# A fused attention and gated feed-forward kernel: the first quad's weight sums made in another stage, wider rows in a DRAM layout, and a new list of steps

## The chip, the cores and the metric

One core of one Trainium2 chip. The metric is the device time of one execution, in microseconds (us). Three executions of the kernel before took 906.19, 904.66 and 909.0 us; the median is 906.19.

## What is computed

Attention for 8 batches and 8 heads over 576 positions of 64 values (heads 0 to 3 see the last 32 positions, heads 4 to 7 every 32nd position before their own), then a gated feed-forward layer over the 8 x 576 = 4608 tokens.

```python
rel = pos[:, None] - pos[None, :]
mask_local = (rel >= 0) & (rel < 32)
mask_strided = (rel >= 0) & (pos[None, :] % 32 == pos[:, None] % 32)
scores = np.where(masks, scale * (q @ k.T), -1e9)        # per batch and head
attn = softmax(scores)
x = (attn @ v).transpose(0, 2, 1, 3).reshape(4608, 512)
gate = 1.0 / (1.0 + np.exp(-(x @ w_gate)))               # w_gate, w_val: 512 x 1536
val = x @ w_val
out = (gate * val) @ w_out                               # w_out: 1536 x 512
```

## The kernel before

**Blocks and stages.** The tokens lie in nine blocks of 512 columns. Every operand of the feed-forward part is split into a high part (rounded to the type fp32r) and a low part (what is left), and a product is made as high x high + high x low + low x high, so a 128 x 128 weight tile against 512 columns gives three matmuls. Blocks 0 to 2 are computed plainly (steps `g`, `v`, `o`). Blocks 3 and 4, 5 and 6, 7 and 8 are computed as pairs, each in two stages, by a scheme that needs seven products of sums where eight would be plain ones. In the first stage of a pair TensorE makes the gate and value products of half the features at a time (`G` and `V`, line 1075, into the banks `p` and `d`); ScalarE copies `p` out (`c`, L1097), VectorE adds `d` (`ad`, L1102), ScalarE makes the sigmoid (`sg`, L1107 and L1110), VectorE multiplies (`mu`, L1116 and L1119) and forms the sums and differences of hidden values that the second stage takes (`ta` to `td`, L1274). In the output stage ScalarE casts a hidden value to its high part (`hx`, L1288), VectorE subtracts for the low part (`hy`, L1292; `hyp` is the same on GpSimd) and TensorE runs `Oa` and `Ob` (L1303). By TensorE's order the first pair's stages run to 494.6 and 554.6 us of the profiled execution, the second pair's output stage begins near 677.

The third pair's gate and value products use a deeper scheme, in four "quads" (n, m): 26 products (`bp`, L1238) of weight sums with x sums. The weight sums are made ahead of time: `bl` loads the 16 words of a quad (128 x 128 each), `bu` makes 33 sums of two words (L1195 on GpSimd; `buv` on VectorE), `bh` casts four of them at a time to a high part on ScalarE (L1203), `bw` makes the low part (L1207, VectorE; `bwp` GpSimd) and `bd` stores both (L1214). The x sums are `xq`, with casts (L1166) and low parts `xw` (L1169; `xwp` on GpSimd). `z` (L726) copies the left-over columns of the attention's output together for them.

**Beside that** run the attention pieces of the pairs to come: scores `S`, masks `M` (L497), softmax steps (`A`, `D`, `U`, `E`, `N`, `W`), transposes `B` (L590), values `X` (L628, L656), and copies out of the banks (`H`, `L`, `R`; L705 is in `R`). The weight sums of the ordinary pairs (`pa`, `pb` L983, `ph`, `pw` L992) are stored to DRAM (`sets`), and TensorE's weights come back from there through the ring: 186 loads of 512 KB, 84 of them from `sets` (`r`, `load_group`).

**What sets the order.** Nothing chooses at run time. `ORDER` lists 3,417 steps by name; each step issues its instructions, and every engine, SyncE with the DMA queue among them, runs its own in the order of the list, waiting by semaphores for what others make. So a step listed between two others stands in the queue of its engine there, and whatever follows on that engine waits with it.

## Time and profile before

| | us | share |
|---|---|---|
| median of three runs | 906.19 | |
| profiled execution | 908.58 | |
| its span in the trace | 906.8 | |
| TensorE busy | 887.7 | 98% |
| VectorE busy | 723.9 | 80% |
| ScalarE busy | 502.2 | 55% |
| GpSimd busy | 464.4 | 51% |
| DMA, mean of 16 engines | | 74% |

The busy time of TensorE is counted from a matmul's begin to its modelled end; matmuls overlap, so a short wait can hide in it. The shares are means over stages of different kinds. The waits of TensorE, and the engines that release them, are the first thing to read.

### The profile page before, as it was taken

What the parts mean: (1) busy time and instruction counts of PE and PEld (TensorE: products, weight loads), DVE (VectorE), ACT (ScalarE), POOL (GpSimd) and SP (SyncE); (2) the same over time, 40 slices, a digit from 0 to 9 for tenths busy, and PEclk for the clock granted to TensorE, in tenths of its full rate; (3) what the DMA queues carried; (4) which work ended last, traced back from release to release, by engine and by line L of the source; (5) the groups of instructions that cost most, each with busy time, mean ns of one, the idle gap of its engine ahead of it and who ended that gap; (6) DMA issues with size and microseconds to landing.
All of it is one profiled execution on the core that took longest, in us unless ns stands there. A gap on an engine that the chain in (4) does not pass through costs nothing.

```text
span 906.8 us, 18603 instructions
## 1 busy us (share of the span) xinstructions
PE 887.7 (98%) x7014; PEld 720.1 (79%) x7014; DVE 723.9 (80%) x1134; ACT 502.2 (55%) x928; POOL 464.4 (51%) x603
## 2 busy tenths in 40 slices
PE   8999989999999999999999999999999999999998
PEld 5788768888887878888778888888877868888886
DVE  6888778776877888789888996768689978998863
ACT  5888754424545555565656664554465554454453
...
GB/s 345 329 238 178 278 280 211 150 199 219 157 227 135 215 215 263 248 310 298 293 266 249 264 237 284 293 292 288 302 321 210 192 281 250 330 234 291 215 213 129
DMA packets 130937, 225.12 MB, mean 248 GB/s; under 512 B 9760, under 2 KB 67104, under 8 KB 130080
## 3 DMA queue, kind: packets, MB, share of 16 engines
...
q8 instruction: 55, 0.90, 0.4%
...
## 4 chain that ended last, share of the span: by engine, by line
PE 80%; DVE 7%; ACT 4%; DMA 4%; issue 2%; POOL 1%; SPq 1%; DVEq 0%; ACTq 0%; POOLq 0%
PE oc L1303 18%; PE p L1075 12%; PE d L1075 10%; PE g L735 9%; PE v L735 8%; PE o L766 7%; PE q L1238 6%; PE qa L1238 2%; PE qv L1238 1%; PE qg L1238 1%; PE s L478 1%; PE x L656 1%; DVE pt L590 1%; DMA quad<-qw 1%; DMA sets<-w 1%
## 5 line engine op out<-in xcount | busy, mean ns | idle before, releaser
L1075 PE MATMUL p<-xs,ring 128*128 128x512 f32 x576 | 141.8, 392 | 4.6 <-issue 2.0
L1075 PEld LDWEIGHTS p<-xs,ring 128*128 128x128 f32 x576 | 107.0, 188 | 28.4 <-issue 2.4
L1075 PE MATMUL d<-xs,ring 128*128 128x512 f32 x432 | 108.4, 395 | 0.1
L1303 PE MATMUL oc<-hh,ring 128*128 128x512 f32 x312 | 104.2, 390 | 0.9 <-DMA ring<-osets 0.5
L1075 PEld LDWEIGHTS d<-xs,ring 128*128 128x128 f32 x432 | 81.9, 190 | 18.2 <-DVE hid L1102 0.5
L766 PE MATMUL o<-w,hh 128*128 128x512 f32 x288 | 90.5, 395 | 0.0
L735 PE MATMUL v<-xh,w 128*128 128x512 f32 x256 | 85.3, 391 | 0.7 <-DVE sb L497 0.6
L735 PE MATMUL g<-xh,w 128*128 128x512 f32 x256 | 85.7, 392 | 0.2 <-ACT e L743 0.2
L983 POOL TENSOR_TENSOR sum<-sum 128x128 f32<-128x128 f32 x100 | 55.6, 558 | 47.3 <-DMA quadw<-sum 32.1
L1195 POOL TENSOR_TENSOR qu<-qw 128x128 f32<-128x128 f32 x96 | 48.7, 525 | 58.9 <-DMA qw<-quadw 45.7
L1303 PE MATMUL oc<-ops,ring 128*128 128x512 f32 x288 | 72.3, 389 | 0.0
L1288 ACT CAST hh<-hid 128x512 fp32r<-128x512 f32 x78 | 47.3, 620 | 40.1 <-PE oc L1303 29.9
L1303 PEld LDWEIGHTS oc<-hh,ring 128*128 128x128 f32 x312 | 58.6, 188 | 13.8 <-DMA ring<-osets 0.9
L1292 DVE TENSOR_TENSOR hl<-hid,hh 128x512 fp32r<-128x512 f32 x55 | 51.9, 962 | 16.8 <-ACT hh L1288 15.2
L1303 PEld LDWEIGHTS oc<-ops,ring 128*128 128x128 f32 x288 | 54.1, 188 | 11.3
L1303 PE MATMUL oc<-hl,ring 128*128 128x512 f32 x156 | 61.3, 393 | 0.8 <-DVE hl L1292 0.6
L766 PEld LDWEIGHTS o<-w,hh 128*128 128x128 f32 x288 | 52.9, 188 | 11.5 <-ACT hh L755 0.2
L978 POOL TENSOR_TENSOR sum<-w 128x256 f32<-128x256 f32 x49 | 40.5, 846 | 39.4 <-DMA sets<-sum 18.8
L590 DVE STREAM_TRANSPOSE pt<-sb 32x320 f32<-32x320 f32 (+1 forms) x112 | 55.4, 495 | 2.9
L735 PEld LDWEIGHTS v<-xh,w 128*128 128x128 f32 x256 | 48.0, 188 | 11.8 <-DVE sb L497 1.0
L735 PEld LDWEIGHTS g<-xh,w 128*128 128x128 f32 x256 | 48.0, 188 | 10.7 <-ACT e L743 0.5
L766 PE MATMUL o<-w,hl 128*128 128x512 f32 x144 | 56.1, 390 | 0.0
...
## 6 DMA issues: line engine op xcount, KB each, us to landing
ring<-sets SPq DMA_DIRECT2D x84, 512.0 KB, 5.6
ring<-osets SPq DMA_DIRECT2D x63, 512.0 KB, 4.5
ring<-quad SPq DMA_DIRECT2D x39, 512.0 KB, 4.8
raw<-in_w_all SPq DMA_DIRECT2D x36, 512.0 KB, 6.1
...
```

What stands on the lines that cost most here:

```text
L478: nc.tensor.matmul(sc[j % len(sc)][g * m : (g + 1) * m, j // len(sc) * BANK + (s - lo) * kk : j // len(sc) * BANK + (s - lo + 1) * kk], q[ ...
L590: nc.vector.transpose(dst[band * LB : (band + 1) * LB, at : at + n, col * LB : (col + 1) * LB], src[part * LB : (part + 1) * LB, x : x + n ...
L735: nc.tensor.matmul(o, w, x, start=first and n == 0, stop=last and n == len(todo) - 1)
L766: nc.tensor.matmul(acc[k][i], h[:, i * P : (i + 1) * P], w, start=f == 0 and n == 0, stop=f == NF - 1 and n == 2,)
L978: by.tensor_tensor(to, part(wh[f][i], c), part(wl[f][i], c), op=ALU.add)
L983: by.tensor_tensor(u[:, to], u[:, x], u[:, y], op=op)
L1075: nc.tensor.matmul(to, w[:, (wi * 2 + c) * P : (wi * 2 + c + 1) * P], x[xi][:, c], start=p in (1, 2, 5) and c == j == 0, stop=c == 1 and j ...
L1195: by.tensor_tensor(to, a, word_slot(w, b), op=ALU.add if op == "+" else ALU.subtract)
L1238: nc.tensor.matmul(quad_bank(m, CHAIN[p]), w[:, wi], xi, start=p in CHAIN_STARTS and j == 0, stop=j == 2, skip_group_check=True)
L1288: nc.scalar.copy(ops[q, p][0], hidden_tile(k, q, KEPT[str(p)]))
L1292: by.tensor_tensor(hl, hidden_tile(k, q, KEPT[str(p)]), hh.bitcast(F32), op=ALU.subtract)
L1303: nc.tensor.matmul(chains[m, at], w[:, (wi * 2 + m) * P : (wi * 2 + m + 1) * P], x[xi], start=p in (1, 2, 5) and q == j == 0, stop=q == PA ...
```

## The change

1. `sets` is laid out so that the two halves (`i`) of a set lie side by side: a ring load reads rows of 4 KB where it read two of 2 KB for each partition.
2. The first quad's words are loaded into two places of the x operands (`w5_0`, `w5_1`) that hold nothing during the first pair's output stage, and its sums are made in three more (`w6_0`, `w6_1`, `w4_0`), instead of in the tiles `xh`, `hh` and `hl` that the output stage uses. The other three quads stay in those tiles.
3. `ORDER` is listed anew. The first quad's load, sums, casts, low parts and stores stand in the first pair's output stage, where they stood in its gate and value stage. In 224 of the 3,417 steps the engine is another: 65 word sums, 24 output low parts and 10 low parts of x sums go from GpSimd to VectorE, 17 output low parts and 23 low parts of words from VectorE to GpSimd, and the rest are a few of each kind. The steps themselves and TensorE's order stay as they were.

```diff
 ORDER = """
...
-v2.10 xd3.0.1 xh3.0.6 xl3.0.6 E11 N11 W11 s2.10 xlp3.1.1 xl3.0.5 g2.11 m2.10 x2.10 po4 B11.3 LV11 v2.11 xlp3.0.2 r3 r2 r4 bl0.0 xdv3.0.2 y2.10 oh2.9.0
...
+hyp3.4.1 ad3.5.0.7 B19.0 pwp5.2.1 B19.2 xh5.1.2 xl5.1.2 G3.5.4 c3.5.1.7 ad3.5.1.7 xh5.0.1 B19.1 V3.5.4 bl0.0 sg3.5.4 mu3.5.4 sg3.5.7 mu3.5.7 G3.5.3
...
-bw1.1.3 hx5.0.1 hy5.0.1 c5.5.0.6 G5.5.7 c5.5.1.6 V5.5.7 xw15 bd1.1.3 ad5.5.0.2 G5.5.5 xu23 bh1.1.4 bw1.1.4 xw23 c5.5.0.7 G5.5.4 r88 bd1.1.4 bu1.1.21
...
+c5.5.0.1 r85 r84 r87 G5.5.2 sg5.4.3 B23.2 X23.1 G5.5.6 bd1.1.2 ad5.5.1.2 V5.5.5 r86 ad5.5.0.2 sg5.5.2 bh1.1.5 bwp1.1.5 V5.5.6 mu5.4.3 c5.5.0.6 mu5.5.2
...
@@ -934,7 +935,7 @@
 
     def sets_of(q):
         if q not in sets:
-            sets[q] = dram.tile([P, 2 * 7, 2, 2, P], F32, name=f"sets{q}")
+            sets[q] = dram.tile([P, 7, 2, 2, 2, P], F32, name=f"sets{q}")
         return sets[q]
 
     def plain_sets(q):
@@ -942,8 +943,8 @@
         for i in range(2):
             for n, w in ((0, wh), (1, wl)):
                 a, b = (w[f][i].bitcast(F32).rearrange("p (k c m) -> p k c m", k=2, c=2) for f in (2 * q, 2 * q + 1))
-                nc.sync.dma_start(sets[q][:, 7 * i : 7 * i + 2, n], a)
-                nc.sync.dma_start(sets[q][:, 7 * i + 2, n], b[:, 1])
+                nc.sync.dma_start(sets[q][:, :2, i, n], a)
+                nc.sync.dma_start(sets[q][:, 2, i, n], b[:, 1])
             for p in W_RAW:
                 k, f = divmod(W_RAW[p], 4)
                 if f // 2 == q % 2:
@@ -996,7 +997,7 @@
         if i == 2:
             to = [out_set(q)[:, 3:7, n, c] for n in range(2)]
         else:
-            to = [sets_of(q)[:, 7 * i + 3 : 7 * i + 7, n, c] for n in range(2)]
+            to = [sets_of(q)[:, 3:7, i, n, c] for n in range(2)]
         nc.sync.dma_start(to[0], h.bitcast(F32))
         nc.sync.dma_start(to[1], u)
 
@@ -1028,7 +1029,7 @@
                 for q in range(2):
                     ring[k, x, 2 * y + q] = to[:, q]
             else:
-                nc.sync.dma_start(to.bitcast(F32), sets[x][:, SLOT[y] : SLOT[y] + 8 : 7].rearrange("p s h c m -> p s (h c m)"))
+                nc.sync.dma_start(to.bitcast(F32), sets[x][:, SLOT[y]].rearrange("p s h c m -> p s (h c m)"))
                 ring[k, x, y] = to
 
     x_set, diffs = {}, {}
@@ -1169,8 +1170,16 @@
         by.tensor_tensor(x_spot(X_AT[n][1]), x_word(f"x{n}"), x_spot(X_AT[n][0]).bitcast(F32), op=ALU.subtract)
 
     def load_words(n, m):
-        w = quad[n, m] = {"w": work.tile([P, 16, P], F32, tag="xh", name=f"qw{n}_{m}")}
-        nc.sync.dma_start(w["w"], quad_words(n, m).rearrange("p q c k m -> p (q c k) m"))
+        from_ = quad_words(n, m).rearrange("p q c k m -> p (q c k) m")
+        if (n, m) == (0, 0):
+            w = quad[n, m] = {i: pool.tile([P, 8, P], F32, tag=f"w5_{i}", name=f"qw{n}_{m}_{i}") for i in range(2)}
+            for i in range(2):
+                nc.sync.dma_start(w[i], from_[:, 8 * i : 8 * i + 8])
+        else:
+            t = work.tile([P, 16, P], F32, tag="xh", name=f"qw{n}_{m}")
+            w = quad[n, m] = {i: t[:, 8 * i : 8 * i + 8] for i in range(2)}
+            nc.sync.dma_start(t, from_)
+        w["sums"] = {}
 
     def word_slot(w, name):
         n = int(name[1:])
@@ -1178,12 +1187,20 @@
             return word_slot(w, ("r3", "r11")[n])
         if name[0] == "r":
             k, f = divmod(n, 4)
-            return w["w"][:, f // 2 * 8 + k % 2 * 4 + f % 2 * 2 + k // 2]
+            return w[f // 2][:, k % 2 * 4 + f % 2 * 2 + k // 2]
         u, at = (5, n % 4 + n // 24 * 2) if n >= 20 else divmod(n, 4)
-        if u not in w:
-            tag = ("hh0", "hl0", "hh1", "hl1", "hh2", "hl2")[u]
-            w[u] = work.tile([P, 4, P], F32, tag=tag, name=f"qu{len(quad)}_{u}")
-        return w[u][:, at]
+        return word_place(w, u)[:, at]
+
+    def word_place(w, u):
+        if u not in w["sums"]:
+            if len(quad) == 1:
+                t = pool.tile([P, 8, P], F32, tag=("w6_0", "w6_1", "w4_0")[u // 2], name=f"qu1_{u // 2}")
+                for j in range(2):
+                    w["sums"][u // 2 * 2 + j] = t[:, 4 * j : 4 * j + 4]
+            else:
+                tag = ("hh0", "hl0", "hh1", "hl1", "hh2", "hl2")[u]
+                w["sums"][u] = work.tile([P, 4, P], F32, tag=tag, name=f"qu{len(quad)}_{u}")
+        return w["sums"][u]
 
     def word_sum(n, m, j, by=nc.gpsimd):
         w = quad[n, m]
@@ -1195,20 +1212,20 @@
             by.tensor_tensor(to, a, word_slot(w, b), op=ALU.add if op == "+" else ALU.subtract)
 
     def word_high_at(w, u):
-        at = (0, 6)[u % 2]
-        return w["w"][:, at : at + 4].bitcast(F32R)
+        return w[u % 4 // 2][:, u % 2 * 4 : u % 2 * 4 + 4].bitcast(F32R)
 
     def word_high(n, m, u):
         w = quad[n, m]
-        nc.scalar.copy(word_high_at(w, u), w[u])
+        nc.scalar.copy(word_high_at(w, u), word_place(w, u))
 
     def word_low(n, m, u, by=nc.vector):
         w = quad[n, m]
-        by.tensor_tensor(w[u].bitcast(F32R), w[u], word_high_at(w, u).bitcast(F32), op=ALU.subtract)
+        x = word_place(w, u)
+        by.tensor_tensor(x.bitcast(F32R), x, word_high_at(w, u).bitcast(F32), op=ALU.subtract)
 
     def store_quad(n, m, u):
         w = quad[n, m]
-        for part, x in ((0, word_high_at(w, u).bitcast(F32)), (1, w[u])):
+        for part, x in ((0, word_high_at(w, u).bitcast(F32)), (1, word_place(w, u))):
             for p, at, size in ((4 * u, 0, 4),) if u < 5 else ((20, 0, 2), (24, 2, 2)):
                 to = place_of(m, p)
                 nc.sync.dma_start(quad_set(n)[:, to // 4, part, to % 4 : to % 4 + size], x[:, at : at + size])
```

Below, names are the program's tiles; a number behind a name tells buffers of one tag apart, and `a<-b,c` is output and inputs.

ScalarE, in the second pair's gate and value stage, around the copy `z` (`xraw8`). Before:

```order
L705 COPY xr6_5732<-x23_7795 128x2x18
L705 COPY xr6_5732<-x23_7795 128x2x12
L705 COPY xr6_5732<-x23_7795 128x2x2
L726 COPY xraw8_7845<-xr0_80 128x4x128
L726 COPY xraw8_7845<-xr2_2135 128x4x256
L726 COPY xraw8_7845<-xr6_5732 128x4x128
L1203 CAST qw1_1_7604<-qu4_2_7608 128x512
L1166 CAST xs7_pt_7858<-xraw8_7845 128x512
L1166 CAST xs7_vv_7880<-xraw8_7845 128x512
L1203 CAST qw1_1_7604<-qu4_3_7611 128x512
L1288 CAST hh5_0_1_7885<-hid5_0_6757 128x512
L1097 COPY e5_5_6_7889<-p05_5_7743 128x512
```

After:

```order
L1111 ACTIVATE e5_5_1_7803<-e5_5_1_7803 128x512
L1219 CAST qw1_1_7559<-qu4_5_7564 128x512
L1098 COPY e5_5_6_7872<-p05_5_7751 128x512
L706 COPY xr6_5718<-x23_7821 128x2x18
L706 COPY xr6_5718<-x23_7821 128x2x12
L706 COPY xr6_5718<-x23_7821 128x2x2
L727 COPY xraw8_7878<-xr0_80 128x4x128
L727 COPY xraw8_7878<-xr2_2269 128x4x256
L727 COPY xraw8_7878<-xr6_5718 128x4x128
L1098 COPY hid5_13_7885<-p15_5_7758 128x512
L1098 COPY e5_5_7_7893<-p05_5_7751 128x512
```

What moved: the copy `e5_5_6<-p05_5`, which empties TensorE's bank `p`, stood behind `z` and five casts, and stands ahead of `z` now; the casts of `xs7` come later.

VectorE, in the first pair's gate and value stage, around the gate product `hid3_10<-e3_4_4,p13_4` (step `mu3.4.4`). Before:

```order
L590 STREAM_TRANSPOSE pt6_2_5809<-sb6_2_5716 32x9x32
L590 STREAM_TRANSPOSE pt6_2_5809<-sb6_2_5716 32x10x32 x2
L1102 TENSOR_TENSOR hid3_11_5722<-hid3_11_5722,d13_4_5669 128x512
L1207 TENSOR_TENSOR qu1_4_4813<-qu1_4_4813,qw0_0_4329 128x512
L1274 TENSOR_TENSOR hid3_7_5380<-hid3_6_5083,hid3_5_5045 128x512
L1102 TENSOR_TENSOR e3_4_6_5714<-e3_4_6_5714,d03_4_5656 128x512
L1116 TENSOR_TENSOR hid3_10_5682<-e3_4_4_5826,p13_4_5649 128x512
L1119 TENSOR_TENSOR hid3_10_5682<-hid3_10_5682,e3_4_1_5689 128x512
L1207 TENSOR_TENSOR qu1_5_4547<-qu1_5_4547,qw0_0_4329 128x512
L1119 TENSOR_TENSOR hid3_11_5722<-hid3_11_5722,e3_4_6_5714 128x512
```

After:

```order
L591 STREAM_TRANSPOSE pt6_2_5746<-sb6_2_5655 32x10x32 x5
L591 STREAM_TRANSPOSE pt6_2_5746<-sb6_2_5655 32x9x32 x2
L591 STREAM_TRANSPOSE pt6_2_5746<-sb6_2_5655 32x10x32
L1103 TENSOR_TENSOR hid3_11_5642<-hid3_11_5642,d13_4_5613 128x512
L1103 TENSOR_TENSOR e3_4_6_5650<-e3_4_6_5650,d03_4_5606 128x512
L1117 TENSOR_TENSOR hid3_10_5603<-e3_4_4_5762,p13_4_5596 128x512
L1309 TENSOR_TENSOR hl3_1_1_5879<-hid3_2_4731,hh3_1_1_5878 128x512
L1120 TENSOR_TENSOR hid3_10_5603<-hid3_10_5603,e3_4_1_5637 128x512
L1120 TENSOR_TENSOR hid3_11_5642<-hid3_11_5642,e3_4_7_5691 128x512
```

What moved: the low parts of the quad's words (`qu1_4`, `qu1_5`) and one hidden sum are gone from here, and the first low part of the output stage (`hl3_1_1`) has come in behind the gate product.

VectorE, in the first pair's output stage (`hl3_...` and `ops3` are low parts that TensorE takes). Before:

```order
L1292 TENSOR_TENSOR hl3_0_2_6157<-hid3_0_4519,hh3_0_2_6156 128x512
L1292 TENSOR_TENSOR hl3_1_2_6139<-hid3_3_4811,hh3_1_2_6138 128x512
L1292 TENSOR_TENSOR ops3_5975<-hid3_5_5045,ops3_5975 128x512
L1274 TENSOR_TENSOR hid3_14_6040<-hid3_13_5983,hid3_12_5961 128x512
L1292 TENSOR_TENSOR hl3_4_2_6182<-hid3_10_5682,hh3_4_2_6181 128x512
L1274 TENSOR_TENSOR hid3_13_5983<-hid3_14_6040,hid3_13_5983 128x512
L1274 TENSOR_TENSOR hid3_5_5045<-hid3_6_5083,hid3_7_5380 128x512
L1292 TENSOR_TENSOR hl3_5_2_6193<-hid3_13_5983,hh3_5_2_6192 128x512
L1274 TENSOR_TENSOR hid3_12_5961<-hid3_14_6040 128x512
L1292 TENSOR_TENSOR ops3_5975<-hid3_2_4764,ops3_5975 128x512
L600 STREAM_TRANSPOSE pt6_3_6055<-sb6_3_5956 32x12x32 x2
```

After:

```order
L1309 TENSOR_TENSOR ops3_5625<-hid3_5_4989,ops3_5625 128x512
L1309 TENSOR_TENSOR hl3_0_2_6110<-hid3_0_4490,hh3_0_2_6109 128x512
L1062 TENSOR_TENSOR xs5_5_1_6118<-xd5_0_0_6043,xs5_5_0_6045 128x512
L1309 TENSOR_TENSOR hl3_4_2_6124<-hid3_10_5603,hh3_4_2_6123 128x512
L1309 TENSOR_TENSOR ops3_5625<-hid3_8_5367,ops3_5625 128x512
L1212 TENSOR_TENSOR qw0_0_1_6015<-qw0_0_0_6014,qw0_0_1_6015 128x128
L1212 TENSOR_TENSOR qw0_0_1_6015<-qw0_0_1_6015 128x128
L1212 TENSOR_TENSOR qu1_2_6129<-qw0_0_1_6015,qw0_0_0_6014 128x128
L1212 TENSOR_TENSOR qu1_2_6129<-qw0_0_1_6015 128x128
L1050 TENSOR_TENSOR xd5_0_2_6142<-xraw6_5682 128x512
L1309 TENSOR_TENSOR hl3_5_2_6150<-hid3_13_5978,hh3_5_2_6149 128x512
L1212 TENSOR_TENSOR qu1_0_6082<-qw0_0_0_6014,qu1_0_6082 128x128
```

What moved: hidden sums (`hid3_...<-hid3_...`) were made between the low parts; now word sums of the quad (`qw0_0_...`, `qu1_...`, 128x128) and a difference of x operands (`xd5_0_2`) stand there.

## Rows read from the trace of the kernel before

**Rows 1.** Page, part 1: busy us (share of the span) and instructions.

```profile
PE 887.7 (98%) x7014; PEld 720.1 (79%) x7014; DVE 723.9 (80%) x1134; ACT 502.2 (55%) x928; POOL 464.4 (51%) x603
```

**Rows 2.** Chain that ended last: start us, us, engine and line, count.

```profile
846.02 57.13 PE oc L1303 x252
```

**Rows 3.** Page, part 5: count, then busy us, mean ns of one, idle and releaser.

```profile
L1303 PE MATMUL oc<-hh,ring 128*128 128x512 f32 x312 | 104.2, 390 | 0.9 <-DMA ring<-osets 0.5
```

**Rows 4.** TensorE's waits: line, waited for, us in total, times, longest.

```profile
PE x L656 <- DMA vv<-in_v_s: 2.4, 1, 2.4
PE p L1075 <- issue: 2.0, 1, 2.0
...
PE p L1075 <- DVE hid L1116: 1.4, 1, 1.4
PE p L1075 <- ACT e L1097: 1.2, 1, 1.2
...
PE x_a L628 <- ACT xr L705: 0.9, 1, 0.9
PE oc L1303 <- DVE hl L1292: 0.6, 2, 0.4
PE v L735 <- DVE sb L497: 0.6, 1, 0.6
...
PE oc L1303 <- ACT hh L1288: 0.4, 1, 0.4
```

**Rows 5.** ScalarE from 662 us in time: start, us, line, operation, tiles.

```profile
662.49 2.11 ACT L726 COPY xraw<-xr 128x512 f32<-128x512 f32 x3
...
667.09 0.60 ACT L1097 COPY e<-p 128x512 f32<-128x512 f32 x1
```

**Rows 6.** VectorE from 474 us in time.

```profile
474.12 0.69 DVE L1207 TENSOR_TENSOR qu<-qu,qw 128x512 fp32r<-128x512 f32 x1
...
475.92 0.68 DVE L1116 TENSOR_TENSOR hid<-e,p 128x512 f32<-128x512 f32 x1
```

**Rows 7.** VectorE at 323.8 us, with the idle time before it.

```profile
323.78 1.18 DVE L992 TENSOR_TENSOR sum<-sum,sumh 128x512 fp32r<-128x512 f32 x1 [1.00 <-ACT sumh L988]
```

**Rows 8.** GpSimd and then ScalarE, from 731 us in time.

```profile
731.44 1.74 POOL L1169 TENSOR_TENSOR xs<-xs,xs 128x512 fp32r<-128x512 f32 x1
...
733.20 0.62 ACT L1166 CAST xs<-xs 128x512 fp32r<-128x512 f32 x1 [3.24 <-POOL xs L1169]
```

**Rows 9.** Page, parts 3 (packets, MB) and 6 (count, KB each, us to landing).

```profile
q8 instruction: 55, 0.90, 0.4%
...
ring<-sets SPq DMA_DIRECT2D x84, 512.0 KB, 5.6
ring<-osets SPq DMA_DIRECT2D x63, 512.0 KB, 4.5
```

**Rows 10.** Windows: us, busy of PE, PEld, DVE, ACT, POOL (count), clock, DMA share, GB/s.

```profile
446.00:450.10 4.10, 4.10 (x130) 3.31 (x129) 4.03 (x7) 3.23 (x7) 1.93 (x2) 1.00 1.00 338
...
452.60:456.60 4.00, 4.00 (x11) 3.16 (x12) 2.31 (x4) 2.14 (x5) 1.55 (x2) 0.58 0.37 113
...
494.60:554.60 60.00, 60.00 (x426) 49.40 (x424) 55.89 (x78) 36.39 (x68) 20.32 (x16) 1.00 0.72 249
554.60:600.00 45.40, 45.40 (x239) 37.44 (x236) 27.13 (x43) 20.27 (x34) 18.75 (x37) 1.00 0.86 298
668.00:737.00 69.00, 67.29 (x289) 53.66 (x289) 61.93 (x70) 37.62 (x70) 44.51 (x29) 1.00 0.68 229
```

**Rows 11.** Groups of VectorE from 494.6 to 554.6 us, shapes apart.

```profile
L1274 DVE TENSOR_TENSOR hid<-hid,hid 128x512 f32<-128x512 f32 x6 | 7.3, 1228 | 0.0
...
L1274 DVE TENSOR_TENSOR hid<-hid 128x512 f32<-128x512 f32 x3 | 2.0, 681 | 0.0
```

**Rows 12.** Groups of the whole span, shapes apart.

```profile
L1195 POOL TENSOR_TENSOR qu<-qw 128x128 f32<-128x128 f32 x96 | 48.7, 525 | 58.9 <-DMA qw<-quadw 45.7 <-PE p L1075 12.7
...
L983 DVE TENSOR_TENSOR sum<-sum 128x128 f32<-128x128 f32 x44 | 15.7, 358 | 1.6 <-DMA quadw<-sum 0.5
```

More of the change, by code (lines that the diff above doesn't have):

```diff
@@ new lines @@
+c3.2.0.6 LV15 G3.2.7 pw2.2.1 pd2.2.1 LQ16 E15 N15 c3.2.0.7 ad3.2.0.7 V3.2.7 Y15 c3.2.1.7 ad3.2.1.7 G3.2.4 sg3.2.4 V3.2.4 pa3.2.0 pb3.2.0 sg3.2.7
+V3.2.3 hx3.2.1 r19 r20 pa3.2.1 G3.2.3 ph3.2.0.0 pwp3.2.0 S16.1 LQ17 pb3.2.1 ta3.1 W15 B15.0 B15.1 R14 B15.3 B15.2 H14 X15.1 Y16 mu3.2.7 G3.3.1
+ad3.2.0.3 mu3.2.4 M16.0 A16 sg3.2.3 D16 ad3.2.1.3 c3.3.0.1 M16.1 H15 G3.3.2 ad3.3.0.2 U16 hy3.2.1 LV16 V3.3.1 c3.3.1.1 G3.3.6 mu3.2.3 r21 r23 E16 N16
+W16 ph3.2.1.1 c3.3.0.6 B16.2 V3.3.6 c3.3.1.6 tav3.2 pwp3.2.1 pd3.2.1 V3.3.2 pa4.2.1 ad3.3.1.2 pb4.2.1 tbv3.1 tc3.2 r22 G3.3.5 G3.3.7 c3.3.0.7 B16.1
@@ new lines @@
+r98 hx5.0.7 hy5.0.7 Oa5.3.5 hyp5.4.5 Ob5.4.5 Ob5.5.5 hx5.1.7 r99 xq17 r100 xu16 tdv5.0 ok5.1.6 Ob5.0.7 hx5.2.7 Oa5.4.5 Oa5.5.5 ok5.0.6 Oa5.0.7 tbv5.5
+xu23 hx5.3.7 td5.1 hx5.5.7 hyp5.5.7 xu1 hy5.1.7 Oa5.1.7 hx5.4.7 Ob5.1.7 xu0 xu5 hx5.0.3 os3.0.7 hy5.2.7 hy5.3.7 Oa5.2.7 Ob5.2.7 hy5.4.7 tdv5.5 hx5.1.3
+hy5.1.3 Oa5.3.7 Ob5.3.7 hy5.0.3 r102 r101 r103 xqv7 xqv15 Ob5.4.7 Ob5.5.7 Oa5.4.7 hx5.2.3 hy5.2.3 ok5.0.5 Oa5.0.3 ok5.1.5 oa5.1.7 os5.1.7 Oa5.1.3
+Oa5.5.7 hx5.3.3 tdv5.2 oa5.0.7 Ob5.0.3 Ob5.1.3 hx5.4.3 xwp0 hx5.5.3 hx5.0.4 hy5.0.4 Ob5.2.3 Oa5.2.3 hyp5.3.3 hx5.1.4 hyp5.4.3 Oa5.3.3 xw23 Oa5.0.4
```

299 lines of the change are left out of this document (146 added, 153 removed).

## The prediction

> **What bounds the kernel now.** I read the share of each engine first, then what TensorE waited for, then the stages in windows, and last the neighbourhood of each wait. TensorE is busy for 887.7 of 906.8 us [rows 1]. The steps that run on it stand in the same order in both lists, with the same shapes, so its work is a constant of this change. What can move is the time in which it stands still: 19.1 us by the busy row. A stop costs a little more than its idle figure: matmuls of 512 columns start every 57.13 / 252 = 0.227 us [rows 2], while one counts as busy for 0.39 us [rows 3], so 0.16 us of each stop hides in "busy". The stops that are named [rows 4]: 2.4 us for a value load (at 130 us), 2.0 us with nothing named (452), 1.4 for VectorE's gate product (476), 1.2 for a copy by ScalarE (667), 0.9 for ScalarE's left-over copy (279), 0.6 for a masked score (325), 0.6 and 0.4 for operands of the output products. The other 9.6 us are start-up, shorter waits and the changes between small and large matmuls; most of these repeat. So the best case is about 2% and no edit can gain more; the worst has no such bound, because any engine can be made late.
>
> The profiled execution took 908.58 us (span 906.8), 2.4 us above the median of the three runs, 906.19. I work out differences on the trace and apply them to the median.
>
> **The change, part by part.** Five of the stops stand behind steps that the new list puts elsewhere.
>
> At 667 TensorE needs a bank that ScalarE empties with the copy `c5.5.0.6`. That copy ran at 667.09, behind the three copies of `z` (2.11 us from 662.49) and five casts [rows 5]. In the new list it stands ahead of `z` and of all five. TensorE then needs nothing that is late there: 1.2 + 0.16 us go. Late next could be `c5.5.1.6`, now behind `z`: its bank is wanted one product of 1.36 us after the other's, about when the copies end, so I count nothing for it; it would cost up to 0.7.
>
> At 476 TensorE waits for the gate product `mu3.4.4`, which VectorE ran at 475.92. Ahead of it stood a low part of the first quad's words, at 474.12 [rows 6], and a hidden sum. Neither stands there now: two starts, 1.2 us of the 1.4, go, half of them because the quad's work left this stage.
>
> At 279 the left-over copy `R5` stood behind the exponential's table load that `D7` makes; now it stands before it. 0.9 us go [rows 4]. At 325 the mask of piece 9 stood behind `pw5.0.0`, 1.18 us that began 1.0 us late on ScalarE [rows 7]; now that step comes after the second masked score and the softmax steps. 0.6 us go.
>
> At 734 ScalarE waited 3.24 us for GpSimd's `xwp0` and the two last casts of the output operands stood behind that wait [rows 8]. Now `hx5.5.4` is listed 12 TensorE steps earlier and GpSimd holds one low part in that stretch instead of six. I count 0.8 us: 0.4 for the cast and 0.4 of the 0.6 for low parts [rows 4].
>
> Sum: 1.2 + 1.2 + 0.9 + 0.6 + 0.8 = 4.7, and 0.16 for each of five stops, 0.8: 5.5 us.
>
> The value load at 130 stays: the store group `pl4` is still ahead of it on SyncE's queue, and only one load of queries (`LQ0`) changes place with it. Bounds 0 and 2.4 us; I take 0.
>
> The longer rows: 84 loads of 512 KB land in 5.6 us from `sets`, where loads of the same size with 4 KB rows, from `osets`, take 4.5 [rows 9]. So each may land 1.1 us earlier. But no wait of TensorE names a load from `sets` [rows 4], so this is hidden and I take 0; the bounds are 0 and what the crowded stretch below is worth.
>
> What is added is in the first pair's output stage, 494.6 to 554.6. VectorE is busy for 55.89 of 60 us there, 4.1 idle [rows 10]. In the list it gets 17 word sums of 128 columns (0.358 each by its nearest row, 6.1), 6 low parts of words (0.68 as the plain sum of 512 columns, 4.1), two low parts and one difference of operands (0.68 each, 2.0), and it loses one output low part (0.7) and three hidden sums (0.68 to 1.23 us, so 2.9) [rows 11, 12]: 8.6 us more. GpSimd gets eight word sums more, 0.525 each [rows 12], 4.2 us. Beside GpSimd VectorE is slower: a hidden sum took 1.228 us in one form and 0.681 in the other in this stage [rows 11], 0.55 more, and I put that down to one GpSimd operation beside it, 1.74 at its slow pace [rows 8]. For 4.2 us of sums that is 4.2 x 0.55 / 1.74 = 1.3. If the list were kept to the place, VectorE would end 8.6 - 4.1 = 4.5 us late, and with the slowing 5.8; with no idle time used up, 9.9. From below it is nothing, when the idle time and what VectorE runs ahead swallow it. I take 1.5 us, near the lower end: its idle time there is waiting for ScalarE's casts, which shrinks by itself once VectorE is behind, and the next stage has 18.3 us of VectorE idle [rows 10] into which the tail can slip. ScalarE gains six casts but is idle for 23.6 of the 60 us. The quad's stores also move into this stage; its DMA share is 0.72 [rows 10].
>
> The Trainium skill (SBUF — State Buffer, section Who interferes with whom) speaks against this place: VectorE with two SBUF operands and a GpSimd operation that reads SBUF exclude each other, and the loser waits for the whole instruction. By that rule GpSimd's 4.2 us cost VectorE 4.2, not 1.3, and the stage would be 2.9 us later at its upper end; the two forms above (0.681 and 1.228) agree in direction and show a part of the price.
>
> The second output stage (from 668) has its x sums and low parts moved from GpSimd to VectorE, 44.51 us busy on GpSimd and 61.93 on VectorE before [rows 10]. That is 12 operations more on VectorE, 8.2 us at 0.68, against less slowing: 13 operations fewer on GpSimd, at 0.55 each 7.2. I take 0; the bounds are 8.2 more and 7.2 less, and half of either is hidden by the idle 7.1 us.
>
> Net: 5.5 - 1.5 = 4.0 us off.
>
> **The rivals.** *The stop with no releaser goes too.* At 452.6 TensorE had stood for 2.0 us in the middle of a group of six, nothing named [rows 4]. Just before, from 446 to 450.1, the 16 DMA engines were busy all the time (share 1.00), and TensorE had run 130 matmuls in those 4.1 us, most of them small [rows 10]. Instructions come by DMA too: queue 8 has 55 packets and 0.90 MB, 16 KB each [rows 9]. I read it as an instruction block that came late behind the loads. After the idle time the clock was granted at 0.58 on average from 452.6 to 456.6 [rows 10], that is, at the lower level (1.2 GHz) for most of it: its 11 matmuls took 4.0 us instead of 11 x 0.227 = 2.5, so the stop costs 2.0 + 0.16 + 1.5 = 3.7. For its going: 3 MB of the quad's stores leave this stage and loads of queries are issued earlier. Against: TensorE's instructions are the same, the burst of ring loads stays, and where a block ends shifts only by a few waits. It would give 902.2 - 3.7 = 898.5.
>
> *As many new stops as old ones go.* Every engine's list is new, and the old one too was a list with eight such stops. For it: five of eight stops were between steps that only the list set side by side. Against: the structural part (the quad out of the crowded stage) has no counterpart. New stops of 4.0 us beside the 1.5 already counted give 906.2; they may be anything from none to twice the 5.5.
>
> *VectorE sets the end of the first output stage.* The mechanism is the 8.6 us above, in order ahead of the low parts that TensorE needs every 1.36 us. For it: VectorE at 93% there. Against: no wait of TensorE in that stage now. Price 5.8 to 9.9, middle 7.9: 906.2 - 5.5 + 7.9 = 908.6, slower than before. It decides once VectorE is more than 5.5 us late.
>
> **How the numbers follow.** Likeliest: five stops go, the output stage costs 1.5: 906.2 - 4.0 = 902.2, own range 899.5 to 905 (chance 0.40). Stop at 452 gone too, 898.5: 0.17. New stops, 906.2: 0.26. VectorE late, 908.6: 0.17. Half a per cent, 4.5 us, is about what a measurement of this kernel can tell from no change. Faster than 901.66 are the second case and 0.45 of the first, 0.17 + 0.18 = 0.35. Slower than 910.72 are the upper end of the VectorE case (its price beyond 9.9, by the idle time that a late VectorE makes on ScalarE) and the tail of the new stops, 0.05 + 0.07 = 0.12. The rest, 0.53, is within. The range runs from 897 to 909.5: below it is a third of the second case, above it the tops of the last two.
>
> **What would show it.** Right: no wait of `p` on ScalarE's copy near 667, of `p` on VectorE's gate product near 475, of `x_a` on the left-over copy near 279; TensorE idle near 15 us; VectorE busy over 58 us in the first output stage and at most two short waits of `oc` in it. Wrong: waits of `oc` on `hl` or `ops` of several us between 495 and 555 (VectorE late), a list of waits as long as now with other names (new stops), or no wait without a releaser and no stretch at the lower clock (then 898).

## The result, and the profile after

The changed kernel takes 894.9 us, the median of six executions (893.14 to 897.84), against 907.25 us for six of the kernel before. The ratio is 0.9859, with a 95% interval from 0.9822 to 0.9897: 12.4 us less by the medians, 9 to 16 by the interval, where 4.0 were forecast. It lies below the forecast's range of 897.0 to 909.5. The profiled executions, on which the rest is worked out, have spans of 906.8 and 891.9 us, 14.9 apart, so some 2.5 us of that difference belong to these two executions. Line numbers move by 1 behind the list and by 17 behind `load_words`.

What TensorE waits for in the changed kernel, the whole list (line, waited for: us in total, times, longest), against [rows 4]:

```profile
PE unread L857 <- POOL ones L851: 1.5, 1, 1.5
PE d L1076 <- issue: 1.1, 1, 1.1
PE x L657 <- issue: 0.5, 1, 0.5
PE t L575 <- issue: 0.5, 1, 0.5
PE x L629 <- DVE pt L591: 0.4, 1, 0.4
PE g L736 <- DVE xl L697: 0.3, 1, 0.3
PE oc L1320 <- DMA ring<-osets: 0.3, 1, 0.3
PE x L657 <- ACT pt L614: 0.2, 1, 0.2
PE x L657 <- ACT pt L612: 0.2, 1, 0.2
```

None of the named stops of [rows 4] is left, neither the five of the sum nor the value load; the stop without a releaser is 1.1 us, not 2.0. Busy time shows the same: 882.6 of 891.9 us, where it was 887.7 of 906.8 [rows 1], so TensorE stands still for 9.3 us, not 19.1.

Two views put the gain in its places. First the kernel before, cut at TensorE's first and last matmul of a stage: the first pair's gate and value stage, its output stage, the second pair's output stage (columns as in [rows 10]):

```profile
360.08:494.47 134.39, 130.90 (x1229) 106.37 (x1228) 116.04 (x193) 79.39 (x147) 88.05 (x128) 0.99 0.85 275
494.47:553.62 59.15, 59.15 (x377) 48.69 (x375) 55.44 (x78) 35.84 (x67) 20.45 (x16) 1.00 0.71 246
...
677.39:738.23 60.84, 59.13 (x253) 46.90 (x252) 55.63 (x59) 32.51 (x60) 39.66 (x27) 1.00 0.63 214
```

and the same three of the changed kernel:

```profile
355.20:484.86 129.66, 128.52 (x1229) 105.30 (x1228) 115.66 (x189) 76.76 (x141) 79.06 (x109) 1.00 0.81 268
484.86:544.83 59.97, 59.69 (x377) 48.53 (x375) 57.10 (x91) 38.91 (x75) 26.44 (x28) 1.00 0.86 293
...
667.34:724.47 57.13, 57.13 (x254) 47.30 (x253) 53.21 (x72) 32.53 (x58) 24.65 (x16) 1.00 0.73 236
```

The part ahead of them went from 360.1 to 355.2 us (4.9 less; by the same list and code up to there it took 355.4 in `words_on_dve` and 359.9 in `words_twice`), the gate and value stage lost 4.7, the output stage that took up the quad grew by 0.8, and the second output stage lost 3.7. The rest (1.3 and 1.2 less, 0.1 more) is small. VectorE's busy time in the first output stage grew by 1.7 us (55.44 to 57.10), where the prediction added up 8.6.

The loads and the stop without a releaser. In the page of the changed kernel ring loads from `sets` still take 5.5 us to land, after 5.6 [rows 9], although their rows are longer:

```profile
ring<-sets SPq DMA_DIRECT2D x84, 512.0 KB, 5.5
ring<-osets SPq DMA_DIRECT2D x63, 512.0 KB, 4.9
```

The windows around the stop at 446 us have the same picture as [rows 10] had at 446 to 450: 128 matmuls in 3.7 us with the DMA engines busy throughout, then 1.1 us of nothing, but no lower clock behind it.

```profile
441.40:445.10 3.70, 3.70 (x128) 2.95 (x127) 3.60 (x6) 2.15 (x3) 3.23 (x5) 1.00 1.01 307
445.10:446.70 1.60, 0.46 (x3) 0.03 (x2) 1.53 (x3) 1.36 (x3) 1.60 (x2) 1.00 1.02 401
```

### The profile page after: what moved, and what is told of

It is laid out like the page before. It is cut to its first block, busy times and chain, and to the rows that moved or that the text cites. A ratio compares the mean times of both kernels' runs of the same rounds, so it can differ in the third digit from the quotient of the medians.

```text
span 891.9 us, 18574 instructions
## 1 busy us (share of the span) xinstructions
PE 882.6 (99%) x7014; PEld 720.2 (81%) x7014; DVE 719.4 (81%) x1187; ACT 500.9 (56%) x928; POOL 438.3 (49%) x550
## 4 chain that ended last, share of the span: by engine, by line
PE 92%; DMA 3%; DVE 3%; ACT 1%; issue 1%; SPq 0%; POOL 0%; DVEq 0%; ACTq 0%
PE oc L1320 17%; PE p L1076 13%; PE o L767 11%; PE g L736 11%; PE v L736 11%; PE d L1076 10%; PE q L1255 6%; PE qa L1255 3%; PE s L479 1%; PE qv L1255 1%; PE qg L1255 1%; PE x L657 1%; DMA raw<-in_w_all 1%; DMA ring<-osets 1%; PE x L629 1%
## 5 line engine op out<-in xcount | busy, mean ns | idle before, releaser
L984 POOL TENSOR_TENSOR sum<-sum 128x128 f32<-128x128 f32 x108 | 57.5, 533 | 46.6 <-DMA quadw<-sum 32.4
L979 POOL TENSOR_TENSOR sum<-w 128x256 f32<-128x256 f32 x48 | 37.8, 808 | 41.8 <-DMA sets<-sum 28.9
L1309 DVE TENSOR_TENSOR hl<-hid,hh 128x512 fp32r<-128x512 f32 x61 | 47.1, 791 | 9.6 <-ACT hh L1305 9.6
L1212 POOL TENSOR_TENSOR qu<-qw 128x128 f32<-128x128 f32 x60 | 31.8, 548 | 44.3 <-DMA qw<-quadw 36.5
```

The source lines that it names most:

```text
L979: by.tensor_tensor(to, part(wh[f][i], c), part(wl[f][i], c), op=ALU.add)
L984: by.tensor_tensor(u[:, to], u[:, x], u[:, y], op=op)
L1212: by.tensor_tensor(to, a, word_slot(w, b), op=ALU.add if op == "+" else ALU.subtract)
L1309: by.tensor_tensor(hl, hidden_tile(k, q, KEPT[str(p)]), hh.bitcast(F32), op=ALU.subtract)
```

## The experiments

Executions of one kernel differ: 31 of the kernel before, taken beside the first four experiments, lie between 901.16 and 915.01 us. So stops of 1 or 2 us are read from the traces, and the time decides from some 3 us on. Each kernel has one trace, of one execution, and some stops differ between executions of the same steps; where they do, it is said. Stops are given "start to start": the time from one matmul's start to the next, less the usual 0.227.

### One load past another

```diff
-... wu11.0 fB1.2.2 fS1.3 LQ0 wu10.2 ... fX1.2 fV1.3 pl0 ...
+... wu11.0 fB1.2.2 fS1.3 wu10.2 ... fX1.2 fV1.3 LQ0 pl0 ...
```

> The kernel before with one step moved: the first load of queries, LQ0, stands behind fV1.3, the value load that TensorE waited 2.4 us for at 130 us, instead of ahead of it. Theory A (the value load was late because 608 KB of queries were issued just ahead of it on the same queue): the wait of x on vv disappears, TensorE's stop of 2.56 us (start to start) at 130 falls under 0.5, and the time falls by 2 to 2.6 us, about 904.5. Theory B (the load is late behind the stores of the weights, which stay ahead of it): the wait stays over 1.5 us, and the time is the same as before. A price could show as a later wait of s on qk; by A there is none.

907.23 us, ratio 0.9995 (0.9972 to 1.0018); the time does not show the exchange. The wait on the value load is gone from the trace, and the load lands sooner after its issue (KB, us), before and here:

```profile
vv<-in_v_s SPq DMA_DIRECT2D x1, 384.0 KB, 5.4
```

```profile
vv<-in_v_s SPq DMA_DIRECT2D x1, 384.0 KB, 3.4
```

That is theory A for the landing: 4.8 to 5.4 us in the seven traces in which `LQ0` stands ahead of this load, 3.1 to 5.0 in the eleven in which it stands behind. For the stop one trace does not settle it. The start-up was longer in this execution (granted clock 0.86 over the first 30 us, 1.00 in the profile of before), and TensorE came to the load 2.0 us later. With `LQ0` ahead the stop was 2.6 us in the kernel before, 1.4 in `layout`, 1.0 in `old_no_quad`, 0.7 in `five_moves`, and there was none in `before_shift`, `old_plain` and `old_no_quad_room`; with `LQ0` behind there was none but 1.0 in `after_old_layout` and 0.7 in `words_twice`.

### Five moves in the old list

```diff
-... G5.5.6 ad5.5.1.2 ... hx5.0.1 hy5.0.1 c5.5.0.6 ...
+... G5.5.6 c5.5.0.6 ad5.5.1.2 ... hx5.0.1 hy5.0.1 ...
-... M7.0 D7 R5 ...
+... M7.0 R5 D7 ...
-... H8 pw5.0.0 Y9 Z9 S9.0 M9.0 pd5.0.0 M9.1 ... E9 ...
+... H8 Y9 Z9 S9.0 M9.0 M9.1 ... E9 pw5.0.0 pd5.0.0 ...
-... ad3.4.1.3 bw0.0.4 tav3.2 G3.4.3 ... mu3.4.4 ...
+... ad3.4.1.3 G3.4.3 ... mu3.4.4 bw0.0.4 tav3.2 ...
-... xwp0 xu6 ... hx5.4.4 hy5.4.4 Oa5.4.4 os5.0.3 hx5.5.4 hyp5.5.4 ...
+... hx5.4.4 hy5.4.4 hx5.5.4 xwp0 xu6 ... Oa5.4.4 os5.0.3 hy5.5.4 ...
```

> The kernel before with the five local moves that the prediction's sum rests on: c5.5.0.6 right behind its product, R5 ahead of D7, pw5.0.0 (with its store) behind the softmax steps of piece 9, bw0.0.4 and tav3.2 behind mu3.4.4, and hx5.4.4, hy5.4.4, hx5.5.4 ahead of xwp0 with hyp5.5.4 on VectorE. Nothing else changes: the quad stays in the gate and value stage and the rows stay 2 KB. Theory A (each stop belongs to the place of one step and they add): the stops near 279, 325, 476, 667 and 734 us are gone and the time falls by 5.5 to 6.5 us, to about 901. Theory B (a stop that is removed comes back at the next step, since the list as a whole is too full there): under 2 us, 905 to 907.

910.19 us, ratio 1.0031 (1.0005 to 1.0056): slower by a little, beyond what either theory had; B is the nearer. The five stops shrank, but the third move made a new one of 5.6 us. TensorE's wait, then ScalarE's timeline (start, us):

```profile
PE g L735 <- ACT e L743: 5.6, 1, 5.6
```

```profile
314.25 0.62 ACT L988 CAST sumh<-sum 128x512 fp32r<-128x512 f32 x1 [7.92 <-DMA sets<-sumh]
...
316.82 0.60 ACT L743 ACTIVATE e<-g 128x512 f32<-128x512 f32 x1
```

The cast `ph5.0.1.1` writes the tile that `pd5.0.0` stores. With `pw5.0.0` and its store moved back, the cast waited for the store, and the sigmoid behind it in ScalarE's queue waited too.

The same with that place mended, the value load ahead and the start-up's extra matmuls (below):

```diff
-... H8 pw5.0.0 Y9 ... pd5.0.0 M9.1 LV9 y2.6 D9 ph5.0.1.1 pwp5.0.1 pl5 A9 U9 E9 ... s2.8 B9.3 ...
+... H8 Y9 ... M9.1 LV9 y2.6 D9 pl5 A9 U9 pw5.0.0 pd5.0.0 E9 ... s2.8 ph5.0.1.1 pwp5.0.1 B9.3 ...
```

> The kernel before with the single moves put together and mended: the five local moves (pw5.0.0 now right behind U9, and ph5.0.1.1 and pwp5.0.1 listed behind s2.8, so that no cast stands in ScalarE's queue for a tile that waits for the store pd5.0.0), LQ0 behind fV1.3, and the 62 small matmuls in the start-up that shift TensorE's instruction blocks. The quad stays in the gate and value stage, the rows stay 2 KB. Theory A (the change gains by taking away single stops, each due to the place of one or two steps, and each stop of 2 us or more also costs a stretch at the lower clock): stops of 2.6, 1.1, 0.7, 1.6, 1.4, 1.4 and 2.2 us and a stretch at the lower clock of 1.6 us go, up to 1 us comes back as start-up; 896 to 899. Theory B (the gain needs the quad out of the crowded stage, or the list as a whole; single moves only push the stops on): 903 to 908.

910.53 us, ratio 1.0029 (1.0008 to 1.0051), again slower than both theories. The mended move pushed GpSimd's low part `pwp5.0.1` back, the weight sums behind it came late, and VectorE held the low part of these sums ahead of a score's mask (VectorE's timeline):

```profile
327.66 1.18 DVE L997 TENSOR_TENSOR sum<-sum,sumh 128x512 fp32r<-128x512 f32 x1 [4.71 <-ACT sumh L993]
328.76 0.48 DVE L497 TENSOR_TENSOR sb<-s_g,cst 128x320 f32<-128x320 f32 x1
```

So neither of these two moves took that stop away without making another of 5 us. Theory A's rule for the lower clock does not hold in the traces either: behind stops of 2.8 us in `value_first`, 2.6 in `five_moves` (at 454 us) and 2.1 in `load_late` (at 447 us) the clock was granted at 1.00, behind 2.2 in the kernel before and 2.0 in `seven_late` it fell. Without the move:

> The kernel before with the moves that did not cause a new stop: c5.5.0.6 behind its product, R5 ahead of D7, bw0.0.4 and tav3.2 behind mu3.4.4, hx5.4.4, hy5.4.4, hx5.5.4 ahead of xwp0 with hyp5.5.4 on VectorE, LQ0 behind fV1.3, and the shifted instruction blocks; pw5.0.0 and its neighbours stay where they were. By the stops that these moves left in the trace of six_moves_shift: 2.6 (value load), 0.6, 0.9, 0.2, 0.7 and 2.2 with 1.6 at the lower clock are gone, 8.8 us, and 0.7 to 1.6 us come as start-up: theory A 898 to 901. Theory B (moves push stops on): one new stop of 2 us or more, 903 or later.

904.44 us, ratio 0.9951 (0.9929 to 0.9973): 4.5 us less, about half of the 8.8. Neither theory holds whole: there is no new long stop, but next to each place the next step is late. What is left of the four other stops is 0.5 (left-over copy), 0.7 (gate product), 0.5 and 0.6 (the copies) and 0.7 us (low part), start to start. Two that were not moved are longer in this trace: 1.4 us for the masked score at 326, where it was 0.7, and 1.2 for a ring load at 675, where it was 0.7.

### The instruction blocks

```diff
         ones, o = busy_with
+        if n == 1:
+            w = ones.bitcast(BF16)[:64, :64]
+            for _ in range(62):
+                nc.tensor.matmul(o[:64, :64], w, w, start=True, stop=True)
+            return
```

(with the step `J1`, which calls it, behind `J1088` in the list)

> The kernel before with 62 small matmuls of 64 columns, whose result is never read, added in the start-up: 124 more instructions of TensorE, so that its instruction blocks of 256 begin at other places and none covers the whole run of 240 small instructions at 447 us. The trace of before shows a block entered at 446.19, the next one's 16 KB packet on queue 8 at 450.12, and the stop from 450.4 to 452.6. Theory A (the stop is a late instruction block): it is gone, with the stretch at the lower clock behind it, 3.7 us less, and the added matmuls cost 0 to 1.7 us in the start-up, so 903.5 to 905. Theory B (TensorE's queue waits there for something else that the trace does not name, a ring load or a semaphore): the stop stays at about 2 us in the same place of the program, and the time is 906 to 909.

908.22 us, ratio 1.0005 (0.9979 to 1.003): no gain, and by the time theory B. The trace is of the fastest of the ten executions (905.13 us, span 903.4); what the others lost is not on record. In it the stop is gone and no stretch at the lower clock follows, so the mechanism is theory A's. TensorE runs the 120 small matmuls and the group behind them without a break:

```profile
447.60 1.04 PE L478 MATMUL s<-qk 64*32 64x64 f32 x80
448.56 0.99 PE L628 MATMUL x<-pt,vv 64*64 64x96 f32 x40
449.48 1.67 PE L1080 MATMUL p<-xs,ring 128*128 128x512 f32 x6
450.99 1.32 PE L1080 MATMUL d<-xs,ring 128*128 128x512 f32 x5
```

The changed kernel with three matmuls fewer in the start-up:

```diff
-... J576 ... J1088 ... J256 ... J256 ...
+... J512 ... J1024 ... J512 ...
```

> The changed kernel with three fewer matmuls in the start-up's warming (576, 1088, 256 and 256 columns become 512, 1024 and 512): six instructions of TensorE fewer, so that its instruction blocks begin elsewhere. Theory A (the stop of 1.3 us that is left at 446 us is a late instruction block): the block there lasts 5.3 us instead of 3.7 and the stop falls under 0.4; 893.5 to 894.5, hard to tell by time, plain in the trace. Theory B (it is not): the stop stays at 1 to 1.5 us.

895.52 us (891.31 to 896.6), ratio 0.9856 (0.9831 to 0.988), not to be told from the changed kernel by time. The stop fell from 1.3 to 0.3 us start to start: theory A again. Whether the kernel is faster for it can't be told within the spread.

### The longer rows alone, and the change without them

```diff
-sets[x][:, SLOT[y] : SLOT[y] + 8 : 7]
+sets[x][:, SLOT[y]]
```

(with the tile and the stores of `sets` to match, the list as it was; the second kernel is the reverse edit on the changed one)

> The kernel before with only the layout of sets changed, so that a ring load reads rows of 4 KB; the list is the old one. Theory A (the loads were hidden): no more than 1 us, about 906 to 907, though the loads from sets land up to 1.1 us sooner. Theory B (the shorter loads free the DMA engines in the crowded stretches, and so shorten the stop at 452 us that no engine released): that stop falls from 2.2 to under 1 us and the time by 2 to 4 us.

906.51 us, ratio 0.9999 (0.9968 to 1.0029), the stop at 450 us 2.1 us long with the lower clock behind it: theory A.

> The changed kernel with the old layout of sets, so that ring loads read two rows of 2 KB for each partition again. Theory A (the loads are hidden in the new list as in the old): 895 to 896, no wait of TensorE on a load from sets. Theory B (the new list, fuller of DMA in the first output stage, needs the longer rows): waits on ring<-sets of several us, or the stop without a releaser at 446 us longer by 1 us or more; 898 to 902.

896.2 us, ratio 0.9879 (0.9852 to 0.9907). No wait names `ring<-sets`, the stop without a releaser is 0.9 us: theory A, within the spread. The trace is of the slowest of its four executions (901.02 us). At one place of it a load counts: VectorE's first word sum of the second quad waits for its words, and TensorE's wait for a half product's sum behind it is 1.4 us. That this is due to the shorter rows is not shown: in `words_twice`, with the longer ones, the same two waits are 2.4 and 1.7 us.

```profile
555.48 0.29 DVE L1212 TENSOR_TENSOR qu<-qw 128x128 f32<-128x128 f32 x1 [2.16 <-DMA qw<-quadw]
```

### The quad's work in the output stage

The old list without the quad's steps up to the first output stage, then the new list:

```diff
-(new list up to Ob3.0.1)
+(old list up to Ob3.0.1, without bl0.0, bu0.0.*, bh0.0.*, bw0.0.*, bd0.0.*)
+tc3.2 R18 LQ20 tb3.4 xh5.0.2 B19.3 B19.2 B19.1 bl0.0 xh5.0.5
 Ob3.0.1 Ob3.1.1 tav3.5 ... (new list)
```

> The changed kernel's code with a list put together from both: the old list up to the first output stage, but without the first quad's steps; from there the new list, with the quad's steps in the output stage. So the old plain part and the old gate and value stage of the first pair, relieved of the quad's 33 sums, 6 casts, 6 low parts and 3 MB of stores. That stage took 134.4 us in the kernel before and 129.7 in the changed one. Theory A (the quad crowded it): 129.5 to 131.5 us with TensorE's stop at mu3.4.4 under 0.4 us, since the low part of words that stood ahead of it is gone, and the stop without a releaser at 452 under 1.5 us; in all 898 to 901. Theory B (the stage gained by the places of other steps): 132.5 us or more, in all 901 to 904.

908.91 us, ratio 0.9999 (0.9974 to 1.0025), slower than both theories. The two stages in its trace:

```profile
361.36:492.20 130.84, 129.13 (x1229) 105.21 (x1228) 109.56 (x187) 75.78 (x140) 72.31 (x96) 1.00 0.79 258
492.20:559.46 67.26, 61.98 (x377) 49.37 (x375) 61.75 (x94) 38.99 (x75) 31.63 (x34) 0.97 0.77 268
```

The gate and value stage has theory A's time, 130.8 us, and no stop at `mu3.4.4`. But of the 3.6 us that it lost only 1.5 are that stop. The other 2.1 are the stop without a releaser, 1.7 us here (theory A had under 1.5) with no lower clock behind it, and that one varies: in `before_shift`, where the quad is in the stage and this stop is not, the stage takes 130.4 us, and with the new list it takes 128.9 to 132.8 (`words_on_dve`, `words_twice`). So 1.5 us is what taking the quad out is shown to be worth there. The whole is no gain: the output stage takes 67.3 us, with waits for low parts of 5.1 us, though its steps stand as in the changed kernel.

The same cut at the first half product, `V3.0.1`: the old plain part with the new list behind it.

> The changed kernel's code, with the old list for the plain blocks (up to the first half product of the first pair) and the new list from there. The plain part took 360.1 us before the first ring product in the kernel before and 355.2 in the changed one. Theory A (stops add by stage): 359.5 to 361 us in the plain part and the new times after it, so 898 to 901 in all. Theory B (the stages behind make up for a late plain part, since what waits there are loads and other engines): 895 to 897.

897.83 us (894.95 to 899.86), ratio 0.9882 (0.985 to 0.9914): between the theories, nothing settled. In its trace the plain part takes 355.4 us and the value load is not waited for, so the plain part's stops are in part a matter of the execution; by the new list it takes 355.2 to 360.1 us in its eight traces.

More work on VectorE, in two doses:

```diff
-bu0.0.4 bu0.0.1 ... bu0.0.11 ...
+buv0.0.4 buv0.0.1 ... buv0.0.11 ...
```

> The changed kernel with all the first quad's word sums on VectorE in the first output stage, so those that GpSimd makes there move over. Theory A (VectorE has room there: it is waited for by nothing): about 16 sums of 0.28 to 0.41 us more, 5 us, on VectorE, some of it given back since GpSimd no longer runs beside it; TensorE's stops in that stage grow by less than 1 us, 895 to 896. Theory B (the stage has no room left for VectorE, as the prediction priced it): 3 us or more of waits of oc on hl or ops, 898 to 900.

```diff
+            for _ in range(2 if (n, m) == (0, 0) else 1):
                 by.tensor_tensor(to, a, word_slot(w, b), op=...)
```

> The changed kernel with all the first quad's word sums on VectorE in the first output stage and each made twice (the second time over what the first left, so the words of that quad are not the reference's). It adds some 28 sums of 0.28 us to words_on_dve, 8 us, where the first dose lengthened the stage by 1.4 us (61.3 for 60.0). Theory A (with the first dose VectorE's idle time is used up, and each further us shows): the stage takes 67 to 70 us and the time is 903 to 906. Theory B (VectorE still has slack, the first dose only met single low parts): under 64 us, 897 to 900.

897.43 us, ratio 0.9894 (0.9869 to 0.9918), and 908.46 us, ratio 1.0007 (0.9974 to 1.004). Their first output stages:

```profile
484.25:545.58 61.33, 60.56 (x377) 48.24 (x375) 58.00 (x108) 38.45 (x75) 14.38 (x11) 1.00 0.84 286
```

```profile
492.73:564.97 72.24, 65.27 (x377) 50.99 (x375) 67.63 (x140) 38.30 (x75) 14.38 (x11) 0.93 0.71 242
```

With 17 sums taken over from GpSimd VectorE's busy time rises by 0.9 us only, since what ran beside GpSimd is shorter now (four sums of one form took 0.41 us each, now 0.28), and the stage by 1.4. The second dose of 9.6 us lengthens it by 10.9; this trace is of the slowest of ten executions (917.14 us), but the medians too are 11.0 apart. So the first is nearer to theory A, with 1.4 us for its 1, and the second goes past A, part of it at the lower clock (0.93 over the stage): the changed kernel's stage is nearly full, 0.9 us more of VectorE's time shows already.

### What made the room

Eight steps (`tc3.2 R18 LQ20 tb3.4 B19.3 B19.2 B19.1 bl0.0`) stood in a row at the start of the output stage in `old_no_quad`. Spread ahead of it there (with `xh5.0.2`), and put in that row in the changed kernel:

> old_no_quad with eight steps put where the new list has them or near it, ahead of the first output stage instead of in a row at its start: the transposes B19.1 to B19.3, the hidden sums tc3.2 and tb3.4, the copy R18, the query load LQ20 and bl0.0, the load of the quad's words. In old_no_quad the output stage took 67.3 us, with stops of 1.1 and 4.3 us at low parts and a stretch at the lower clock. Theory A (the room for the quad in that stage comes from work of VectorE and GpSimd done ahead of it, and from the words being loaded in time): 60 to 62.5 us, no stop over 1 us, 900 to 903 in all. Theory B (it needs the new list throughout): 65 us or more, 905 to 909.

> The changed kernel with the same eight steps put in a row right ahead of the first output product, as they stood in old_no_quad. Theory A (they make the room): the first output stage grows from 60.0 to 64 us or more by waits of oc on hl, hh or ops, 899 to 903 in all. Theory B (the room is elsewhere in the new list): under 62 us, 895 to 898.

The first gave 907.72 us, ratio 1.0021 (1.0 to 1.0042): its stage is 63.8 us, but the transposes, put ahead of a gate product, made a stop of 4.8 us just before it. Neither theory. The second gave 902.82 us, ratio 0.9967 (0.9947 to 0.9986), its stage 68.0 us: theory A. Its trace pointed to the load among the eight, so load and seven others were moved apart:

```diff
-... V3.5.4 bl0.0 sg3.5.4 mu3.5.4 ... r39 ... xdv5.0.1 r38 Ob3.0.1 ...
+... V3.5.4 sg3.5.4 mu3.5.4 ... r39 ... xdv5.0.1 r38 bl0.0 Ob3.0.1 ...
```

> The changed kernel with one step moved: bl0.0, the load of the quad's words, right ahead of the first output product, so that on SyncE's queue it stands behind the ring loads r39 and r38 instead of ahead of them. In after_late the words landed at 499.2 us (486.4 in the changed kernel) and the wait went from GpSimd (12.7 us) to VectorE (4.1) to TensorE (6.1). Theory A (of the eight steps the load decides: VectorE's order has word sums ahead of low parts, and they wait for it): a stop of oc on hl of 3 to 6 us and a stage of 64 us or more, 899 to 903. Theory B (the seven others did it, by work): under 62 us, 895 to 897.

> The changed kernel with the seven other steps of after_late (tc3.2, R18, LQ20, tb3.4, B19.1 to B19.3) right ahead of the first output product and the load bl0.0 where it was. Theory A (the load decides): the first output stage stays within 60 to 62 us, 895 to 898. Theory B (the work decides): a stage of 64 us or more, 899 to 903.

903.79 us, ratio 0.9953 (0.9921 to 0.9986), and 898.13 us, ratio 0.9878 (0.9842 to 0.9915). One load, one place: the stage takes 67.3 us with the load late and 61.5 with the seven late (one stop of 1.4 at a low part), 60.0 in the changed kernel: theory A in both by the stage, so most of it is the load. The chain in `load_late`, SyncE's queue first (the changed kernel issued the load at 482.34), then the waits of GpSimd, VectorE and TensorE:

```profile
476.58 12.15 SPq L1028 DMA_DIRECT2D ring<-osets  x5
488.78 1.14 SPq L1177 DMA_DIRECT2D qw<-quadw  x2
```

```profile
POOL qu L1212 <- DMA qw<-quadw: 14.1, 1, 14.1
```

```profile
DVE qu L1212 <- POOL qu L1212: 4.8, 1, 4.8
```

```profile
PE oc L1320 <- DVE hl L1309: 5.1, 1, 5.1
```

GpSimd's sums wait for the words, VectorE's word sum for GpSimd's, the low parts stand behind it, and TensorE needs those. Behind the stop the clock is granted at the lower level:

```profile
501.00:504.20 3.20, 3.20 (x8) 2.55 (x9) 3.04 (x8) 0.31 (x1) 0.95 (x1) 0.50 0.69 274
```

## Why the prediction was wrong

The direction, the bound (TensorE's stops, at most some 2%) and the five stops of the sum were right: these five were 1.1, 0.7, 1.6, 1.4 and 1.4 us start to start, 6.2 together, where the sum had 5.5, and none is left in any of the eight traces of the new list (the changed kernel, `after_shift`, `after_old_layout` and the five in which the output stage was changed). The steps that failed put other stops at nothing, or the quad's price too high; all of them err towards too little.

**"Most of these repeat"**, on the 9.6 us that were not named. Start to start, nine short stops of 0.2 to 0.7 us at 99, 125, 317, 601, 679 to 685 and 746 to 752 us, 4.1 together, are gone, and three new ones make 1.3. So 3.2 us net, apart from 0.4 in the output stage, were missed by not working through the short waits as the long ones were. Those at 601, 746 and 752 (1.4) stand in `value_first`, `layout` and `before_shift` too and in no trace of the new list; those at 99 and 125 (0.9) stand in the profile of before alone.

**"I take 0"** for the second output stage, with bounds of 8.2 more and 7.2 less. By the old list it took 59.8 to 60.8 us in these three and the profile of before, by the new one 57.1 in all eight, which is 252 starts of 0.227 us and no stop. Of the 2.7 to 3.7 us less, 1.4 are the casts at 734, for which the sum had 1.0; the other 1.3 to 2.3, the short stops at 679 to 685 among them, were put at nothing.

**"I take 1.5 us"** for the quad in the output stage, with bounds up to 9.9. The stage grew by 0.8, 0.4 of it a ring load, not a low part. The 8.6 us were counted from steps that enter the stage; what else left it was not (transposes of 3.3 us, output sums), and a word sum took 0.32 us on VectorE on the mean, not 0.358. (In the other direction, the list takes two hidden sums off VectorE there, not three.) VectorE's busy time grew by 1.7.

**"The value load at 130 stays ... I take 0."** It was 2.6 us, and the changed kernel's profile has none. The store group `pl4` did stay ahead, as the prediction said; but what had been issued just ahead of the value load was `LQ0`, 608 KB, and that is the step which "changes place with it". Behind the exchange the load lands sooner (`value_first`), so the term was not nothing. But the stop was anything from 0 to 2.6 us by the old list, and the profile of before has the longest: that the whole 2.6 went is luck of the two executions.

**"The stop with no releaser"** was left in the likeliest case, with a chance of 0.17 that it goes. Between the two profiles it went for two thirds: 2.2 and 1.5 us at the lower clock became 1.3 with no lower clock, 2.4 us. The reading as a late instruction block was right (`before_shift`, `after_shift`). That it shrank is not shown to come from the change. TensorE runs the same instructions up to there in six more kernels with the new list, and the stop is 0.6, 1.1, 1.4, 2.0, 2.1 and 2.9 us in them, twice with the lower clock behind it; by the old list with the quad it is 2.1 to 2.8. The shortest and the longest wait (`words_on_dve`, `words_twice`):

```profile
PE d L1076 <- issue: 0.4, 1, 0.4
```

```profile
PE d L1076 <- issue: 2.7, 1, 2.7
```

The next block's packet on queue 8 began 3.9 us after its block was entered before, 3.0 in the changed kernel, 2.2 and 4.6 in these two. What sets that is not settled; the share of the DMA engines was 1.0 in all four. So the prediction's argument against its going stands, and the 2.4 us are luck as well.

Put together: 6.2 + 2.6 + 2.4 + 3.2 - 0.8 = 13.6 of the 14.9 us between the two profiles. Of the 8.4 us that the medians lie beyond the forecast, what these traces have in common is 4 to 5: 0.7 in the five stops, 1.4 at 601, 746 and 752, 1.3 to 2.3 in the second output stage, 0.7 for the quad. How the rest is shared between the value load, the late block and other short waits, which vary from execution to execution, is not shown.

**The rivals.** "VectorE sets the end of the first output stage" had a price of 5.8 to 9.9 us. `old_no_quad` and `load_late` show 7.3 more than the changed kernel's stage, but that agreement is luck, because the condition was another: in `load_late` VectorE stood waiting 4.8 us for words that were loaded late, with no more to do than in the changed kernel. VectorE's own work alone reaches it in `words_twice`, at 12.3. "As many new stops as old ones go" did not come true here, but it is what happened to moves made singly: `five_moves` and `six_moves_shift` each made a stop of some 5 us in moving one of 0.7. Why the new list as a whole made none was not tried step by step. Of the signs named for being right, the three waits are gone, but TensorE's idle time is 9.3 us, not near 15, and VectorE's busy time 57.1, not over 58.
